# One shared transpose for two heads' 64-key tails, values of the tails against zero-padded V, and a planner that prices each change of product kind

## The chip, the cores and the metric

The kernel runs on one core of a Trainium2 chip. The metric is the device time of one execution in microseconds (us). The engines are PE (TensorE, matrix products and transposes), PEld (its weight loads), DVE (VectorE), ACT (ScalarE), POOL (GpSimd) and SP (SyncE, whose queue issues all DMAs here).

## The reference

Block-causal attention over 4 batches, 8 heads, 576 positions and 64 dimensions per head, with blocks of 64 keys, and two feed-forward layers behind it:

```python
scores = scale * np.matmul(q, k.transpose(0, 1, 3, 2))
block_i = pos[:, None] // block          # block = 64
block_j = pos[None, :] // block
scores = np.where(block_i >= block_j, scores, -1000000000.0)
scores = scores - np.max(scores, axis=-1, keepdims=True)
attn = np.exp(scores)
attn = attn / (np.sum(attn, axis=-1, keepdims=True) + 1e-09)
attn_out = np.matmul(attn, v)
...
x = np.ascontiguousarray(attn_out.transpose(0, 2, 1, 3)).reshape(B * S, H * D)   # 2304 x 512
x = _moe_ref(x=x, **moe_kwargs)      # h = x @ w_in; g piecewise quadratic in h; g @ w_out, d_ff = 2048
return _moe2_ref(x=x, **moe2_kwargs) # h = x @ w_in; g = max(0.01 h, h); g @ w_out
```

## The kernel before

**Attention in units.** Two heads make a pair (16 pairs). A pair's 576 queries are split into part "a" (the first 320) and part "b" (the last 256), so there are 32 units, 16 of each part. Inside a unit the queries stand in chunks, `CH = (first query, queries, keys)`: chunks 0, 1, 2 of part a see 64, 192 and 320 keys, chunks 3 and 4 of part b see 448 and 576. Every number of keys is an odd multiple of 64, so each chunk and head ends in a tail of 64 keys that doesn't fill 128 rows. In the first chunk the tail is all there is.

**A unit's steps.** `unit_scores` loads q and k (and the values V), multiplies q by the scale on POOL, and forms scores on PE (line L651). The contraction is over 64 dimensions, so head 0 uses rows 0 to 63 of the array and head 1 rows 64 to 127 side by side. `softmax` masks (L564), takes maxima (L566) on DVE and exponentials on ACT (L573). The probabilities lie with queries on partitions, so `unit_values` transposes them in pieces of 128 keys on PE (L743), copies the result from PSUM to SBUF on ACT (L748) or DVE (L750), and multiplies it with V on PE (L770). There the output has 64 columns for each head, so the two heads use the two halves of the array's columns side by side. For the first four units the division by the row sum is made late, by a broadcast product with the identity (L762). A chunk whose keys don't fill a multiple of 128 has its last 64 columns zeroed by POOL (L667) and its tail transposed as a full piece, for each head apart. `PCOL` says where each chunk's probabilities begin, `TILES` which pieces share one PSUM slot and one copy, `SUMS` which piece meets which columns of the result:

```python
TILES = {"a": [[(0, 0), (1, 0), (2, 0)], [(1, 1), (2, 1), (2, 2)]],
         "b": [[(3, 0), (4, 0), (3, 1), (4, 1)], [(3, 2), (4, 2), (3, 3), (4, 3)], [(4, 4)]]}
SUMS = {"a": [(0, 0, 0, 320), (1, 0, 64, 256), (1, 256, 192, 128)], ...
```

So an a unit has 12 transposes, two copies (640 and 768 columns) and 6 value products, a b unit 18 transposes, three copies (1024, 1024 and 256 columns) and 10 value products. A score or value product in float32 has two rows in the trace, a transpose one.

**Three kinds of product on PE.** Whole-array products (the feed-forward layers' and the transposes), scores (row halves) and values (column halves). The code calls the last two `tiled`.

**The rest.** While attention runs, `h1_block` and `h1_wide` (L877, L887, L855) fill PE with the first layer's products on tokens whose attention is done, w_float (L508 to L523) and `conv_unit` (L925 to L943) unpack and prepare weights on ACT, DVE and POOL. Then come the other products with seven sub-products to a block: L1191 and L1252 (first layer's output), L1068 (second layer's first product), L1252 again (second layer's output).

**What sets the order.** Nothing runs in the order in which it is written. Every step is an `Op` with an engine, a cost in ns and its dependencies. `Plan.schedule` simulates the engines 400 times with random disturbances (`SEED`), keeps the order whose simulated end is earliest, and emits it; each engine then runs its own list in order. PE pays `ENTRY = 105` in this model when it goes from whole-array to tiled products. Where `SLACKS` isn't 0, a product of the kind that PE is in may be taken ahead of one of the other kind. In the first 20 us, expected gaps of PE are filled with products of zeros (L545), after ten such products at the start.

Of the kernel before, what the change touches and what calls it, by code (L numbers as in the profile page):

```python
# [25 lines left out]
SA = 320  # L26
# [41 lines left out]
ENTRY = 105  # L68
SLACKS = (0, 800)
SEED, TRIES = 6, 400  # L70
# [85 lines left out]
class Op:  # L156
    __slots__ = ("eng", "cost", "prio", "fn", "deps", "succ", "need", "ready", "seq", "end", "start", "port", "tiled", "lag")


class Plan:  # L160
# [9 lines left out]
    def op(self, eng, cost, prio, fn, r=(), w=(), port=False, tiled=False, lag=0):  # L170
        o = Op()
        o.port, o.tiled, o.lag = port, tiled, lag
# [33 lines left out]
    def forward(self, prio, slack):  # L206
# [8 lines left out]
        tiled = False  # L215
# [6 lines left out]
        while events:  # L222
# [5 lines left out]
            for e in engines:  # L228
                if free[e] <= t and waiting[e]:
# [3 lines left out]
                    if e == "PE":  # L233
                        if slack and o.tiled != tiled and waiting[e]:
                            other = min((x for x in waiting[e] if ops[x[1]].tiled == tiled), default=None)
# [61 lines left out]
    def late(self, done, extra):  # L297
# [5 lines left out]
        port, tiled = 0, False  # L303
        for o in done:
# [12 lines left out]
            if e == "PE":  # L317
                if o.tiled and not tiled:
                    t += ENTRY
                tiled = o.tiled  # L320
# [52 lines left out]
def fused_kernel(ctx, tc, qk, v, w1, w2, out):  # L373
# [36 lines left out]
    def pe(cost, prio, fn, r, w, tiled=False):  # L410
        plan.op("PE", cost, prio, fn, r, w, tiled=tiled)
# [142 lines left out]
    def softmax(prio, tag, s, parts, late=None):  # L554
# [5 lines left out]
        for c, heads, view, _, _ in ((p[0], p[2], p[3], p[4], p[5]) for p in parts):  # L560
            keys = CH[c][2]
            m = len(heads)
            if c > 0:
                dve(64 * m, prio, lambda view=view, keys=keys: nc.vector.memset(  # L564
                    view()[0:64, :, keys - 64:keys], NEG), [], [s], fixed=60)
# [36 lines left out]
    PCOL = {0: 0, 1: 128, 2: 384, 3: 0, 4: 512}  # L602
    units = {}
    padded = {}
    ROOMS = {0: {"p": [(P1, 0)], "v": (P2, 1536), "qk": (P2, 2560)},
             1: {"p": [(P2, 0)], "v": (P2, 2176), "qk": (P2, 3392)},
             2: {"p": [(C[8], 0), (C[9], 0)], "v": (C[8], 1152), "qk": (C[10], 0)},
             3: {"p": [(C[11], 0)], "v": (C[12], 0), "qk": (C[12], 384)},
             4: {"p": [(C[13], 0), (C[14], 0)], "v": (C[13], 1152), "qk": (C[15], 0)}}

    def unit_scores(pair, part, prio, ring, room_):
# [5 lines left out]
        nv, nqk, npr = (640, 832, 1152) if part == "b" else (384, 640, 768)  # L617
        vt = vs.reg(vo, nv, shape=lambda ap: ap.rearrange("p (j d) -> p j d", d=128))
        if len(own["p"]) == 1:
            ps_, po = own["p"][0]  # L620
            pr = [ps_.reg(po, 2 * npr)] * 2
            part_of = lambda hd, a, e: (pr[hd], (2000 * hd + a, 2000 * hd + e))
            prob = lambda hd, a, e: pr[hd].get()[:, npr * hd + a:npr * hd + e]
        else:
            pr = [ps_.reg(po, npr) for ps_, po in own["p"]]
            part_of = lambda hd, a, e: (pr[hd], (a, e))
            prob = lambda hd, a, e: pr[hd].get()[:, a:e]
# [4 lines left out]
        q0, k0, nq, nk, nj = (SA, 0, SA, SA, 3) if part == "a" else (0, SB, SB, S, 5)  # L632
        x = qk_room[0].reg(*qk_room[1:])
        if part == "a":
            dma(128 * 2 * SA * 4, prio - 8, lambda: nc.sync.dma_start(
                x.get()[:, 0:2 * SA].rearrange("p (c s) -> p c s", c=2), qk[pair][:, :, SB:]), [], [x])
        else:
            dma(128 * 832 * 4, prio - 8, lambda: nc.sync.dma_start(
                x.get(), qk[pair].rearrange("p c s -> p (c s)")[:, 0:832]), [], [x])
# [783 lines left out]
```

## Time and profile before

| | us |
|---|---|
| median of 3 runs | 928.32 (928.02 to 935.54) |
| the profiled execution | 928.28 |
| its span, first to last instruction | 926.5 |
| PE busy in it | 915.6 |
| DVE, ACT, POOL busy | 727.7, 519.6, 293.9 |

The time of an execution has 1.78 us around the span. Engines work side by side, so their busy times don't add up; an engine's busy share says how much of the span it had something to do, and where it is near 100% its own work sets the time. The granted clock of TensorE is 1.000 over the whole span.

### The profile page before, as it was taken

What the parts mean: (1) busy time and instruction counts of PE and PEld (TensorE: products, weight loads), DVE (VectorE), ACT (ScalarE), POOL (GpSimd) and SP (SyncE); (2) the same over time, 40 slices, a digit from 0 to 9 for tenths busy, and PEclk for the clock granted to TensorE, in tenths of its full rate; (3) what the DMA queues carried; (4) which work ended last, traced back from release to release, by engine and by line L of the source; (5) the groups of instructions that cost most, each with busy time, mean ns of one, the idle gap of its engine ahead of it and who ended that gap; (6) DMA issues with size and microseconds to landing.
All of it is one profiled execution on the core that took longest, in us unless ns stands there. A gap on an engine that the chain in (4) does not pass through costs nothing.

```text
span 926.5 us, 18684 instructions
## 1 busy us (share of the span) xinstructions
PE 915.6 (99%) x6818; PEld 827.7 (89%) x6818; DVE 727.7 (79%) x1247; ACT 519.6 (56%) x1014; POOL 293.9 (32%) x490
## 2 busy tenths in 40 slices
PE   9999999999999999999999999999999999999998
PEld 6687887876777878899999999999999999999998
DVE  6998677777777646559989798677879899888977
ACT  7788677787777666653434343344535664434333
POOL 5577787787665400000000040146445000000000
PEclk9999999999999999999999999999999999999999
DMA  8678788788799789656525499987887983544433
GB/s 310 212 224 249 236 281 285 261 275 272 273 315 323 276 263 325 191 172 209 154 84 161 140 348 337 346 290 269 266 279 242 328 269 91 176 132 139 148 91 115
DMA packets 164892, 216.72 MB, mean 234 GB/s; under 512 B 9920, under 2 KB 138432, under 8 KB 164800
## 3 DMA queue, kind: packets, MB, share of 16 engines
q1 hardware_dynamic: 164800, 215.52, 71.8%
q8 instruction: 54, 0.88, 0.4%
q14 instruction: 38, 0.31, 0.1%
HBM read 134.74 MB, written 80.74 MB: 233 GB/s over the span
## 4 chain that ended last, share of the span: by engine, by line
PE 92%; DVE 2%; DMA 2%; ACT 1%; issue 1%; POOL 1%; SPq 0%; POOLq 0%; DVEq 0%; ACTq 0%
PE bank L1252 31%; PE bank L1068 15%; PE bank L855 14%; PE bank L887 7%; PE bank L1191 6%; PE slot L651 5%; PE slot L770 5%; PE slot L743 5%; DMA rg<-gd 1%; DVE ra L976 1%; DMA wcd<-rg 1%; DMA rb<-x1d 1%; ACT rp L573 1%; PE bank L545 1%; PE slot L762 0%
## 5 line engine op out<-in xcount | busy, mean ns | idle before, releaser
L1068 PE MATMUL bank<-rp,w 128*128 128x288 f32 x1344 | 179.7, 294 | 1.2 <-ACT ra L978 0.9
L1068 PEld LDWEIGHTS bank<-rp,w 128*128 128x128 f32 x1344 | 178.1, 188 | 1.8 <-ACT ra L978 1.2
L976 DVE TENSOR_TENSOR ra<-ra,bank 128x288 f32<-128x288 f32 (+2 forms) x280 | 125.8, 488 | 43.7 <-ACT ra L978 21.8
L1252 PE MATMUL bank<-w,rp 128*128 128x256 f32 x1014 | 145.9, 277 | 0.0
L1252 PEld LDWEIGHTS bank<-w,rp 128*128 128x128 f32 x1014 | 129.8, 188 | 0.0
L855 PE MATMUL bank<-ra,w 128*128 128x512 f32 x384 | 100.0, 398 | 0.3 <-DVE rg L838 0.3
L1237 ACT ACTIVATE rp<-ra 128x1024 fp32r<-128x1024 f32 (+1 forms) x48 | 47.5, 991 | 72.5 <-DVE ra L1211 62.7
L855 PEld LDWEIGHTS bank<-ra,w 128*128 128x128 f32 x384 | 70.1, 188 | 17.1 <-issue 2.3
L838 DVE SCALAR_TENSOR_TENSOR rg<-bank,rg 128x512 f32<-128x512 f32 x72 | 49.3, 684 | 38.0 <-ACT rg L837 35.1
L1072 ACT ACTIVATE ra<-ra 128x1152 f32<-128x1152 f32 x32 | 37.3, 1167 | 71.4 <-DVE ra L976 71.4
L1252 PE MATMUL bank<-rp,w 128*128 128x256 f32 x508 | 76.6, 279 | 0.0
L936 POOL TENSOR_TENSOR w<-w 128x128 f32<-128x128 f32 x128 | 66.9, 543 | 26.7 <-DVE w L932 24.7
L1003 POOL TENSOR_TENSOR xs<-xs,rp 128x576 f32<-128x576 f32 x1 | 1.5, 1547 | 212.0 <-DMA xs<-x2d 212.0
L836 ACT ACTIVATE rg<-bank 128x512 f32<-128x512 f32 x72 | 43.1, 598 | 43.2 <-PE bank L855 36.6
L1252 PEld LDWEIGHTS bank<-rp,w 128*128 128x128 f32 x508 | 67.2, 188 | 0.0
L1240 DVE TENSOR_TENSOR rb<-ra,rp 128x1024 fp32r<-128x1024 f32 (+1 forms) x48 | 54.3, 1133 | 3.9 <-ACT rp L1237 0.7
L1252 PE MATMUL bank<-w,rb 128*128 128x256 f32 x294 | 57.0, 277 | 0.0
L887 PE MATMUL bank<-ra,w 128*128 128x256 f32 x352 | 53.6, 289 | 0.0
L855 PE MATMUL bank<-rb,w 128*128 128x512 f32 x192 | 53.1, 398 | 0.0
L887 PEld LDWEIGHTS bank<-ra,w 128*128 128x128 f32 x352 | 45.1, 188 | 3.5 <-issue 2.6
L1252 PE MATMUL bank<-rg,w 128*128 128x256 f32 x280 | 47.7, 279 | 0.0
L1236 ACT ACTIVATE rp<-rp 128x768 fp32r<-128x768 f32 (+1 forms) x33 | 26.4, 803 | 36.2 <-DMA rp<-gd 21.5
(169 smaller groups left out, 1977.6 us busy)
## 6 DMA issues: line engine op xcount, KB each, us to landing
rp<-gd SPq DMA_DIRECT2D x41, 512.0 KB, 4.2
wcd<-w SPq DMA_DIRECT2D x43, 448.0 KB, 4.6
gd<-ra SPq DMA_DIRECT2D x32, 576.0 KB, 4.8
gd<-rg SPq DMA_DIRECT2D x64, 256.0 KB, 3.6
w<-wcd SPq DMA_DIRECT2D x32, 512.0 KB, 5.7
w<-wcd SPq DMA_DIRECT2D x32, 384.0 KB, 5.7
w<-w SPq DMA_DIRECT2D x44, 256.0 KB, 4.6
w<-w SPq DMA_DIRECT2D x16, 512.0 KB, 5.1
```

Of the source, the lines that this page charges most:

```text
L651: nc.tensor.matmul(out, lhsT=x.get()[r, q:q + 128], rhs=x.get()[r, k0 + ka:k0 + kb], start=start, stop=True, skip_group_check=True)
L743: nc.tensor.transpose(s.get()[:, hd, o:o + 128], prob(hd, a, a + 128), ident.get())
L838: dve(512, pv, lambda: nc.vector.scalar_tensor_tensor(gt.get(), ps.get(), 1.0, gt.get(), op0=ALU.max, op1=ALU.min), [ps, gt], [gt])
L855: nc.tensor.matmul(ps.get(), lhsT=win(fc, c, kc), rhs=xview(xt, x, kc), start=(k == 0 and kc == 0), stop=(k == 2 and kc == NKC - 1), skip_ ...
L887: nc.tensor.matmul(ps.get()[:, 256 - j * 256:512 - j * 256], lhsT=win(fc, c, kc), rhs=xview(xt, x, kc), start=(k == 0 and kc == 0 and j == 0),
L936: plan.op("POOL", 430, prio, lambda o=o, a=a, b=b, op=op: nc.gpsimd.tensor_tensor(sl(o), sl(a), sl(b), op=op), [(fx, (a, a + 1)), (fx, (b, ...
L976: dve(cols, prio, lambda: nc.vector.tensor_tensor(out(o), out(a), P[b][1](), op=op), [P[b][0], (slots, (a, a + 1))], [(slots, (o, o + 1))])
L1068: nc.tensor.matmul(ps.get()[:, 0:HALF], lhsT=wc(1, p, cw, li, 128 * kc, 128 * kc + 128), rhs=r.get()[:, cx, kc], start=(k == 0 and kc == 0 ...
L1191: nc.tensor.matmul(ps[t].get()[:, 0:n], lhsT=wc(z, p, cw, li, 128 * t, 128 * t + 128), rhs=x.get()[:, n * zi:n * zi + n], start=(p == 0 an ...
L1237: act(4 * n, pv, lambda tt=tt, ht=ht: nc.scalar.activation(s_(ht, 0, 4), s_(tt, 0, 4), AF.Copy), [tt], [ht], sb=True)
L1240: dve(4 * n, pv, lambda tt=tt, ht=ht, lt=lt: nc.vector.tensor_tensor(s_(lt, 0, 4), s_(tt, 0, 4), bc(s_(ht, 0, 4)), op=ALU.subtract), [tt, ...
L1252: nc.tensor.matmul(ps.get()[:, 256 * t:256 * t + w], lhsT=b if wide else g, rhs=g if wide else b, start=(p == 0 and k == 0 and t == 0), st ...
```

## The change

Head 1's keys are stored in reversed order of blocks, from the host on. Its tail then is the first 64 keys instead of the last, and stands behind head 0's tail in the probabilities, which now lie head beside head for each chunk (`PBASE`). One transpose of 128 columns takes both tails: rows 0 to 63 of the result are head 0's, 64 to 127 head 1's. The tails' value products (`ENDS`) run over all 128 rows, against V that is zero in the other head's rows, so that each head takes only its own. The zeroing of pad columns goes away. The a unit has 9 transposes (6 of `MAINS`, 3 of `TAILS`), copies of 768 and 320 columns and 10 value products; the b unit 16 transposes, two copies of 1024 columns and 12 value products, with the same total of columns as before in both. V comes in two layouts, with 5 blocks of 64 KB for an a unit instead of 3, and 6 for a b unit instead of 5; q and k come in one contiguous piece for each unit.

The planner knows three kinds of product (`mode` 0 whole array, 1 scores, 2 values), pays for each change into a kind, has new costs for the three steps, may take products of the present kind up to 3000 ns ahead of others, and starts from another seed.

```diff
-ENTRY = 105
-SLACKS = (0, 800)
-SEED, TRIES = 6, 400
+SWITCH = (98, 190, 142)
+SLACKS = (0, 1000, 3000)
+SEED, TRIES = 7, 400
...
-                        if o.tiled and not tiled:
-                            o.end += ENTRY
-                        tiled = o.tiled
+                        if o.mode != mode:
+                            o.end += SWITCH[o.mode]
+                        mode = o.mode
...
-    PCOL = {0: 0, 1: 128, 2: 384, 3: 0, 4: 512}
+    PBASE = {0: 0, 1: 128, 2: 512, 3: 0, 4: 896}
...
-        nv, nqk, npr = (640, 832, 1152) if part == "b" else (384, 640, 768)
+        nv, nqk = (768, 832) if part == "b" else (640, 640)
...
+            k = k0 + hd * (nk - CH[c][2])
+            nc.tensor.matmul(out, lhsT=x.get()[r, q:q + 128], rhs=x.get()[r, k + ka:k + kb], start=start, stop=True,
...
-        for c in ((0, 1, 2) if part == "a" else (3, 4)):
-            keys = CH[c][2]
-            a, b_ = PCOL[c] + keys, PCOL[c] + (keys + 127) // 128 * 128
-            for hd in range(2):
-                if a == b_ or padded.get(room_) == part:
-                    continue
-                pool(0, prio - 1, lambda a=a, b_=b_, hd=hd: nc.gpsimd.memset(prob(hd, a, b_), 0.0), [], [part_of(hd, a, b_)], fixed=86)
...
+    MAINS = {"a": [[(1, 0, 0), (2, 0, 128), (2, 1, 256)], []],
+             "b": [[(3, 0, 0), (4, 0, 128), (3, 1, 256), (4, 1, 384)], [(3, 2, 0), (4, 2, 128), (4, 3, 256)]]}
+    TAILS = {"a": [[], [(0, 0, 0), (1, 0, 64), (2, 0, 192)]], "b": [[], [(3, 0, 384), (4, 1, 384)]]}
+    SUMS = {"a": [(0, 0, 0, 64, 256), (1, 0, 256, 192, 128)],
+            "b": [(0, 0, 0, 0, 256), (1, 0, 256, 0, 256), (2, 1, 0, 0, 256), (3, 1, 256, 128, 128)]}
+    ENDS = {"a": [(2, 0, 0, 0, 64), (3, 0, 64, 64, 128), (4, 0, 192, 192, 128)],
+            "b": [(4, 0, 384, 0, 128), (5, 1, 384, 128, 128)]}
...
-                for hd in range(2):
-                    o = 0
-                    for c, j in blocks:
-
-                        a = PCOL[c] + 128 * j
-                        nc.tensor.transpose(s.get()[:, hd, o:o + 128], prob(hd, a, a + 128), ident.get())
-                        o += CH[c][1]
-            pe(2 * m * 0.85 + 15, prio, f, [*dict.fromkeys(pr), ident], [s])
+                for c, b, o in tails:
+                    a = CH[c][2] - 64
+                    nc.tensor.transpose(s.get()[:, b, o:o + 128], prob(c, a, a + 128), ident.get())
+                for c, j, o in mains:
+                    keys = CH[c][2]
+                    for hd in range(2):
+                        a = keys + 64 + 128 * (keys // 128 - 1 - j) if hd else 128 * j
+                        nc.tensor.transpose(s.get()[:, hd, o:o + 128], prob(c, a, a + 128), ident.get())
+            pe((n + 127) // 128 * 109 + 10, prio, f, [*dict.fromkeys(pr.values()), ident], [s])
...
+            for z, h, o, q0, m in ENDS[part]:
+                for hd in range(2):
+                    r = slice(64 * hd, 64 * hd + 64)
+                    nc.tensor.matmul(s.get()[r, 0, q0:q0 + m], lhsT=vt.get()[:, z, r], rhs=pts[1].get()[:, h, o:o + m], start=False,
+                                     stop=True, skip_group_check=True)
+        pe(sum(max(x[4], 100) for x in SUMS[part] + ENDS[part]) * 1.68 + 10, prio, f, [vt] + pts, [s], 2)
...
-    EVAC = {"a": ("act", "dve"), "b": ("act", "dve", "act")}
+    EVAC = {"a": ("act", "dve"), "b": ("act", "dve")}
...
+    for z in range(2):
+        ends[:, :, z, :, z] = vv[:, :, 0, :, z]
```

Line numbers move by one or two. In the changed kernel tails are transposed in L737, whole pieces in L742; value products are L767 (`SUMS`) and L772 (`ENDS`), scores L652, products of zeros L544.

**An a unit on PE, beside the first layer's products.** In the rows, slot is a PSUM slot of attention, bank one of the first layer, rp and w are SBUF rooms. Before, the unit's second group of transposes and its values:

```order
L743 MATMUL slot_128<-ident,rp_1_95 128x128 x6
L887 MATMUL bank_90<-ra_1_934,w_1_891 128x256 x4
L887 MATMUL bank_90<-rb_1_881,w_1_891 128x256 x2
L887 MATMUL bank_90<-rb_1_1158,w_1_891 128x256 x2
L887 MATMUL bank_90<-ra_1_934,w_1_891 128x256 x8
L651 MATMUL slot_128<-w_1_201 128x320 x2
L770 MATMUL slot_129<-rp_1_78,rp_1_95 64x320 x2
L770 MATMUL slot_129<-rp_1_78,rp_1_95 64x256 x2
L770 MATMUL slot_129<-rp_1_78,rp_1_95 64x128 x2
```

Now, at the same stage:

```order
L737 MATMUL slot_112<-ident,rp_1_91 128x128 x3
L888 MATMUL bank_89<-ra_1_944,w_1_680 128x256 x8
L888 MATMUL bank_89<-rb_1_857,w_1_680 128x256 x2
L888 MATMUL bank_89<-rb_1_1137,w_1_680 128x256 x2
L767 MATMUL slot_127<-rp_1_165,rp_1_91 64x256 x2
L767 MATMUL slot_127<-rp_1_165,rp_1_91 64x128 x2
L772 MATMUL slot_127<-rp_1_165,rp_1_91 64x64 x2
L772 MATMUL slot_127<-rp_1_165,rp_1_91 64x128 x4
L652 MATMUL slot_112<-w_1_208 128x320 x2
```

The second group has three transposes instead of six, and the values end in a product of 64 and two of 128 columns.

**A b unit on PE at the same stage.** Before, from its first transposes to its values:

```order
L743 MATMUL slot_129<-ident,rp_1_78 128x128 x8
L887 MATMUL bank_90<-rb_1_881,w_1_638 128x256 x2
L887 MATMUL bank_90<-rb_1_1158,w_1_638 128x256 x2
L743 MATMUL slot_145<-ident,rp_1_78 128x128 x8
L887 MATMUL bank_90<-ra_1_934,w_1_638 128x256 x4
L743 MATMUL slot_128<-ident,rp_1_78 128x128 x2
L887 MATMUL bank_90<-ra_1_934,w_1_638 128x256 x4
L887 MATMUL bank_90<-rb_1_881,w_1_638 128x256 x2
L887 MATMUL bank_90<-rb_1_1158,w_1_638 128x256 x2
L651 MATMUL slot_145<-w_1_155 128x448 x2
L770 MATMUL slot_129<-rp_1_78,rp_1_95 64x256 x8
L770 MATMUL slot_129<-rp_1_78,rp_1_95 64x128 x2
```

Now:

```order
L742 MATMUL slot_111<-ident,rp_1_165 128x128 x8
L888 MATMUL bank_89<-ra_1_944,w_1_488 128x256 x4
L737 MATMUL slot_112<-ident,rp_1_165 128x128 x2
L742 MATMUL slot_112<-ident,rp_1_165 128x128 x6
L888 MATMUL bank_89<-ra_1_944,w_1_488 128x256 x4
L888 MATMUL bank_89<-rb_1_857,w_1_488 128x256 x2
L888 MATMUL bank_89<-rb_1_1137,w_1_488 128x256 x2
L888 MATMUL bank_89<-ra_1_944,w_1_488 128x256 x4
L652 MATMUL slot_111<-w_1_120 128x448 x2
L767 MATMUL slot_127<-rp_1_165,rp_1_91 64x256 x6
L767 MATMUL slot_127<-rp_1_165,rp_1_91 64x128 x2
L772 MATMUL slot_127<-rp_1_165,rp_1_91 64x128 x4
```

The third group of two transposes and its slot are gone, and two of the four tails' transposes with them.

**The opening on PE,** where wz marks the products of zeros and late the late division. Before:

```order
L545 MATMUL bank_90<-wz 128x128 x5
L651 MATMUL slot_128<-rp_1_95 128x320 x2
L743 MATMUL slot_129<-ident,rp_1_95 128x128 x6
L545 MATMUL bank_90<-wz 128x128 x2
L743 MATMUL slot_145<-ident,rp_1_95 128x128 x6
L545 MATMUL bank_90<-wz 128x128 x2
L762 MATMUL slot_128<-ident,latea_198 64x64 x2
L762 MATMUL slot_128<-ident,latea_198 64x128 x4
```

Now:

```order
L544 MATMUL bank_88<-wz 128x128 x6
L652 MATMUL slot_111<-rp_1_91 128x320 x2
L742 MATMUL slot_112<-ident,rp_1_91 128x128 x6
L544 MATMUL bank_88<-wz 128x128 x2
L737 MATMUL slot_127<-ident,rp_1_91 128x128 x3
L544 MATMUL bank_88<-wz 128x128 x2
L652 MATMUL slot_112<-w_1_139 128x64 x2
L652 MATMUL slot_112<-w_1_139 128x192 x2
L652 MATMUL slot_127<-w_1_139 128x320 x2
L759 MATMUL slot_111<-ident,latea_182 64x64 x2
L759 MATMUL slot_111<-ident,latea_182 64x128 x4
L544 MATMUL bank_88<-wz 128x128 x3
```

The third unit's scores stand ahead of the first late division, and there are 23 products of zeros in all where there were 21.

**Counts over the whole order of PE.** Transposes 480 before, 400 now; value products 256 and 352; all other products as many as before. Runs of scores, each entered from another kind: 56 and 46. Runs of values or late divisions: 36 and 36. Returns to whole-array products: 55 and 56.

## Rows read from the trace of the kernel before

**Rows 1.** The page, busy time and share of the span of each engine.

```profile
PE 915.6 (99%) x6818; PEld 827.7 (89%) x6818; DVE 727.7 (79%) x1247; ACT 519.6 (56%) x1014; POOL 293.9 (32%) x490
```

**Rows 2.** Stretches, busy us of PE, PEld, DVE, ACT, POOL, granted clock, DMA share, GB/s.

```profile
0.00:6.50 6.50, 5.45 (x30) 5.22 (x32) 0.17 (x1) 1.49 (x2) 2.92 (x23) 1.00 0.64 185
6.50:46.00 39.50, 36.72 (x298) 26.51 (x296) 36.62 (x76) 33.31 (x111) 22.05 (x37) 1.00 0.82 274
46.00:330.00 284.00, 282.38 (x2021) 218.05 (x2020) 211.78 (x398) 214.32 (x562) 197.99 (x334) 1.00 0.83 270
330.00:747.00 417.00, 415.20 (x2938) 402.42 (x2937) 325.47 (x531) 195.98 (x253) 70.94 (x96) 1.00 0.76 246
747.00:926.50 179.50, 175.89 (x1539) 175.51 (x1538) 153.69 (x244) 74.53 (x89) 0.00 (x0) 1.00 0.46 142
```

**Rows 3.** What PE waited for after 46 us: us in total, times, longest.

```profile
PE slot L743 <- ACT rp L573: 1.1, 1, 1.1
PE bank L1068 <- ACT ra L978: 0.9, 1, 0.9
PE slot L651 <- POOL w L641: 0.6, 1, 0.6
PE slot L651 <- ACT rp L748: 0.6, 1, 0.6
```

**Rows 4.** The chain that ended last, its end: start us, us, what.

```profile
922.93 0.42 DVE ra L976
```

**Rows 5.** Groups of PE by line: transposes (of two groups alike but for the room).

```profile
L743 PE MATMUL slot<-ident,rp 128*128 128x128 f32 x252 | 33.8, 276 | 1.4 <-ACT w L573 0.9 <-ACT rp L573 0.2 <-issue 0.2
```

**Rows 6.** The chain in 196 to 216 us, a stretch where PE never waits.

```profile
199.49 0.75 PE slot L651 x8
...
202.46 0.92 PE bank L855 x4
203.38 0.74 PE slot L651 x4
204.12 1.34 PE slot L770 x12
...
207.50 1.96 PE slot L743 x18
...
210.39 0.95 PE slot L651 x4
211.34 2.10 PE slot L770 x20
213.44 1.12 PE bank L855 x4
```

**Rows 7.** The chain in 12 to 30 us, the opening.

```profile
12.60 0.45 PE bank L545 x4
...
16.52 0.64 PE bank L545 x4
...
25.09 0.85 PE slot L762 x12
```

**Rows 8.** DVE's and ACT's copies from PSUM in 46 to 330 us, by form.

```profile
L750 DVE COPY rp<-slot 128x1024 f32<-128x1024 f32 x15 | 18.4, 1224 | 9.5 <-PE slot L743 9.2
L750 DVE COPY rp<-slot 128x768 f32<-128x768 f32 x12 | 11.4, 948 | 3.8 <-PE slot L743 3.6
...
L748 ACT COPY rp<-slot 128x256 f32<-128x256 f32 x15 | 5.6, 376 | 0.7 <-PE slot L743 0.7
```

**Rows 9.** DMA issues, V's loads: KB each, median us to landing.

```profile
rp<-v SPq DMA_DIRECT2D x8, 320.0 KB, 4.3
...
rp<-v SPq DMA_DIRECT2D x9, 192.0 KB, 4.3
```

**Rows 10.** Two stretches with the fullest DMA, columns as in group 2.

```profile
150.00:167.00 17.00, 16.43 (x135) 13.29 (x136) 11.81 (x23) 12.53 (x37) 13.60 (x24) 1.00 0.90 293
713.00:747.00 34.00, 32.81 (x247) 32.35 (x246) 30.86 (x59) 21.09 (x27) 2.63 (x5) 1.00 0.94 313
```

More of the change, by code (lines that the diff above doesn't have):

```diff
@@ L156 @@
 class Op:
-    __slots__ = ("eng", "cost", "prio", "fn", "deps", "succ", "need", "ready", "seq", "end", "start", "port", "tiled", "lag")
+    __slots__ = ("eng", "cost", "prio", "fn", "deps", "succ", "need", "ready", "seq", "end", "start", "port", "mode", "lag")
 class Plan:
@@ L233, in forward @@
                     if e == "PE":
-                        if slack and o.tiled != tiled and waiting[e]:
-                            other = min((x for x in waiting[e] if ops[x[1]].tiled == tiled), default=None)
+                        if slack and o.mode != mode and waiting[e]:
+                            other = min((x for x in waiting[e] if ops[x[1]].mode == mode), default=None)
                             if other is not None and other[0] <= first[0] + slack:
@@ L317, in late @@
             if e == "PE":
-                if o.tiled and not tiled:
-                    t += ENTRY
-                tiled = o.tiled
+                if o.mode != mode:
+                    t += SWITCH[o.mode]
+                mode = o.mode
             if o.port:
@@ L372, in fused_kernel @@
 @with_exitstack
-def fused_kernel(ctx, tc, qk, v, w1, w2, out):
+def fused_kernel(ctx, tc, qka, qkb, va, vb, w1, w2, out):
     nc = tc.nc
@@ L408, in turn, with pe @@
         return places[i % len(places)]
[L410 to L411 removed]
+    def pe(cost, prio, fn, r, w, mode=0):
+        plan.op("PE", cost, prio, fn, r, w, mode=mode)
     def act(cols, prio, fn, r, w, sb=False, extra=0):
@@ L559, in softmax @@
         i = 0
-        for c, heads, view, _, _ in ((p[0], p[2], p[3], p[4], p[5]) for p in parts):
+        for c, o, heads, view, _, _ in parts:
             keys = CH[c][2]
@@ L563, in softmax, with masked @@
             if c > 0:
-                dve(64 * m, prio, lambda view=view, keys=keys: nc.vector.memset(
-                    view()[0:64, :, keys - 64:keys], NEG), [], [s], fixed=60)
+                def masked(o=o, keys=keys, heads=heads):
+                    if len(heads) == 1:
+                        a = o if heads[0] else o + keys - 64
+                        return flat2(s)[0:64, a:a + 64]
+                    a, d = o + keys - 64, 576 - keys
+                    return flat2(s)[0:64, a:a + 2 * d].rearrange("p (h t) -> p h t", h=2)[:, :, 0:64]
+                dve(64 * m, prio, lambda masked=masked: nc.vector.memset(masked(), NEG), [], [s], fixed=60)
             dve(keys * m, prio, lambda view=view, i=i, m=m: nc.vector.tensor_reduce(
@@ L643, in unit_scores @@
         ready = [x]
-        dma(128 * nj * 512, prio + 20, lambda: nc.sync.dma_start(vt.get()[:, 0:nj], v[pair][:, 0:nj]), [], [vt])
+        dma(128 * nj * 512, prio + 20, lambda: nc.sync.dma_start(vt.get(), (va if part == "a" else vb)[pair]), [], [vt])
         def score(out, c, hd, ka, kb, start):
@@ L685, in f @@
                         score(s.get()[:, hd, o:o + CH[c][2]], c, hd, 0, CH[c][2], i == 0)
-            pe(score_cost(sum(CH[c][2] for c, _ in grp)), prio, f, ready, [s], True)
+            pe(score_cost(sum(max(CH[c][2], 128) for c, _ in grp)), prio, f, ready, [s], 1)
             softmax(prio, f"{n}_{grp[0][0]}", s, [
@@ L728, in unit_values @@
         pts = []
-        for i, blocks in enumerate(TILES[part]):
+        for i, (mains, tails) in enumerate(zip(MAINS[part], TAILS[part])):
             s = slot(ring[0])
             ring.append(ring.pop(0))
-            m = sum(CH[c][1] for c, _ in blocks)
-            pT = P1.reg(4352 if i == 2 else turn("pt", (2304, 3328)), 256 if i == 2 else 1024,
-                        shape=lambda ap: ap.rearrange("p (h t) -> p h t", h=2))
+            pT = P1.reg(turn("pt", (2304, 3328)), 1024, shape=lambda ap: ap.rearrange("p (h t) -> p h t", h=2))
@@ L757, in f @@
             def f():
-                for i, c in enumerate((0, 1, 2) if part == "a" else (3, 4)):
+                for i, c in enumerate(EVERY[part]):
                     r = CH[c][1]
```

101 lines of the change are left out of this document (51 added, 50 removed).

## The prediction

> **What bounds the kernel now.** I read the page's busy times first, then the same by stretches, then what PE waited for, then the chain. PE is busy for 99% of the span, DVE for 79%, ACT for 56% [rows 1]. The stretches say where this holds: from 46 to 747 us PE is busy for 697.6 of 701 us at a granted clock of 1.00 [rows 2], and its two longest waits there are 1.1 and 0.9 us [rows 3]. Until 46 us things stand differently: from 6.5 to 46 us DVE is busy for 36.62 of 39.5 us, and the 36.72 us of PE contain products of zeros, which do nothing [rows 2]. The end is fixed: the last product is done about 922.5 us after the start, then a sum on DVE begins at 922.93 [rows 4] and the stores follow, so that of the 3.6 us without PE after 747 us most is this tail [rows 2]. So a microsecond of PE work taken out between 46 and 330 us, where attention stands between other products, is a microsecond of the end, as long as the products that follow find their data. One taken out of the opening may turn into waiting.
>
> **The change part by part.**
>
> *Transposes.* 18 in a row after whole-array products take 1.96 us in the chain [rows 6], 0.109 us each (their durations of 276 ns overlap [rows 5]). The order has 400 instead of 480: 80 x 0.109 = 8.7 us less on PE, 3 per a unit and 2 per b unit.
>
> *Value products.* The two sizes of units give the price of a column (of both heads side by side) and of the change of kind: 2.10 us for 1152 columns and 1.34 us for 704 [rows 6] are 0.76/448 = 1.70 ns a column, and leave 0.14 us for the entry. The total of columns stays. What is new is the product of 64 columns in each a unit, and more short ones. A product of 128 columns was in both sums and they fit one price, so I price it by its columns. For 64 columns there are two rows, and they disagree. Scores with 64 + 192 columns take 0.75 us, with 448 columns 0.95 us, with 320 columns 0.74 us [rows 6]. Less 1.70 ns a column the latter two leave 0.19 and 0.20 us for the entry; the first leaves 0.75 - 0.435 = 0.31 us, so its product of 64 columns costs 0.12 us more than its columns. The late division has products of 64, 128 and 128 columns in the array's column halves and takes 0.85 us [rows 7]: 0.544 us of columns and an entry of 0.14 leave 0.17 us, and in that lies a change of kind inside the group (its first product contracts over 64 rows, the others over 128), for which the other changes cost 0.14 to 0.20. So nothing is left there for a short product. The bounds are 0 and 0.12 us per a unit, 0 to 1.9 us in all. I take 0, because the late division has the values' column halves and the scores don't.
>
> The Trainium skill ("TensorE: Matmul & The Clock Gate", section "LDWEIGHTS (loading the stationary operand)") says that a weight load takes as many cycles of 1.2 GHz as it has columns. By an estimate from that page two heads' loads of 64 columns, one behind the other, would take 107 ns for each half of a float32 product, and a product of 64 columns would cost twice its columns, 1.7 us in all and a result of 920.3 us with the other terms of the sum below. Its two loads of 128 columns would then take 213 ns in the scores, or 0.43 us for the product of 64, where the row has 0.23 us; so the trace agrees with the rule at most for loads that lie side by side.
>
> *Changes of kind.* Counted in the two orders, entries into scores fall from 56 to 46, at 0.195 us: 1.95 us less. Entries into values stay at 36. Returns go from 55 to 56, at 1.12 - 0.92 = 0.20 us [rows 6]: 0.2 us more. Together 1.75 us less.
>
> *Copies from PSUM.* An a unit's copy on DVE shrinks from 768 to 320 columns: from 948 ns, with 1.08 ns a column between the two forms, to an estimated 465 ns, 0.48 us less [rows 8]. That is 7.7 us of DVE over 16 units. On ACT it grows by 128 columns, and in a b unit a copy of 376 ns goes [rows 8]. After 46 us both lie beside PE (DVE busy 75%, ACT 75% of 46 to 330 us [rows 2]) and are worth nothing by themselves. What is late next is the copy ahead of a b unit's values: the last one had 256 columns on ACT, 376 ns, and now has 1024 on DVE, 1224 ns [rows 8]. In the order shown scores of 448 columns and eight products of the first layer or more stand between, and the first three value products read only the other copy, so I cost it at nothing; where no cover stands, it is 0.85 us for a unit.
>
> *Zeroing, q and k.* 36 small POOL instructions go, and the loads of q and k become one piece of the same size. POOL is busy for 70% of 46 to 330 us [rows 2] and PE waited for it once, 0.6 us [rows 3], so nothing.
>
> *V's loads.* An a unit loads 320 KB instead of 192, a b unit 384 instead of 320 [rows 9]: 16 x 192 KB = 3.1 MB more, issued from SP's queue with all the rest, where loads and stores of the first layer stand behind them. At 293 GB/s [rows 10] that is 10.7 us of transfers if nothing else ran; hidden while DMA has room (share 0.83 in 46 to 330 us [rows 2]). I cost it at nothing and make the other end a rival.
>
> *The opening.* Four a units and one or two b units are transposed before 46 us, 1.5 to 1.7 us of the 8.7. There PE waits for others, and the expected gaps are filled: 21 products of zeros before, 23 now, 0.45 to 0.64 us for two [rows 7]. For a loss speaks that the order has two more of them. Against it speaks that DVE, busy for 93% of that stretch, loses 4 x 0.48 = 1.9 us of copies. Ends: 0 and 1.6 us lost. I take half, 0.8 us.
>
> *Sum.* -8.7 - 1.75 + 0 + 0.8 = -9.65 us against the profiled execution's 928.28 us, which is the median of the runs within 0.04: **918.6 us**. PE's other idle time, 3.4 us from 46 to 747 us [rows 2], I let stand. The whole order is new, so each of them may go and others come.
>
> **The rivals.**
>
> *Short value products are dear.* If each costs what the scores' one does, and the opening keeps nothing, the sum is -8.7 - 1.75 + 1.9 + 1.6 = -6.95: 921.3 us. For it: the only row of a product of 64 columns by itself in a longer group is the scores'. Against it: the late division. The Trainium skill's rule on weight loads, cited above, speaks for this case.
>
> *New waits.* The order was made by a model from other costs, and a b unit's values wait for a copy that is 0.85 us longer. If that copy is bare in five of 16 units, 4.2 us come back: 922.8 us. Against it: PE waited for a copy once, 0.6 us [rows 3].
>
> *More than the sum.* The opening is DVE's, shortens by the whole 1.9 us of its copies, and the longest wait of PE, 1.1 us [rows 3], goes too: -8.7 - 1.75 - 0.3 - 1.1 = -11.85, 916.4 us.
>
> *V's bytes make DMA the bound: slower than before.* In 46 to 330 us 270 GB/s x 284 us = 76.7 MB move [rows 2]; with some 2.5 MB more (the units loaded after 46 us) it is 79.2 MB in 276 us, 287 GB/s. If the queue gives no more than the 270 of now, the stretch lasts 293 us instead of 276, and the time is 918.6 + 17 = 935.6 us; below 277 GB/s it is slower than before. For it: with DMA at 0.90 and 293 GB/s PE lost 0.57 us in 17. Against it: that is more than 287, and 313 GB/s were moved in 713 to 747 us [rows 10].
>
> That the change doesn't do what it says is no case: the order has the 80 transposes less.
>
> **How the numbers follow.** Forecast 0.58, short products dear 0.11, new waits 0.15, more than the sum 0.11, DMA 0.05. A measurement of this kernel tells a change of about 1%, 9.3 us, from none: below 919.0 us is faster, above 937.6 slower. The forecast lies 0.4 us inside faster; of its 0.58, spread over some 1.5 us to each side, I count 0.36 as faster and 0.22 as same. More than the sum is faster; dear products and new waits are the same. Of the DMA case 0.03 is slower, the rest same. Together faster 0.47, same 0.50, slower 0.03. The likeliest single case gives 918.6 all the same. The range goes from 916.0, which takes in the case of more, to 923.0, which takes in that of new waits; beyond lie the worse half of new waits and DMA.
>
> **What would show it.** Right: L737 and L742 have 400 rows with about 0.109 us from one to the next; an a unit's values take 1.34 us in the chain, a b unit's 2.10; PE stays at 99% in 46 to 321 us, and the end of attention (the last L772) and everything behind it come some 10 us earlier; DVE's copies are 465 ns. Wrong: values of 1.46 us in an a unit (short products); waits of L767 or L772 for L748 (copies); PE idle behind loads, or a DMA share of 0.90 with waits (bytes); a start of the first layer's products in the opening that is no earlier, or new idle time at 390 or 745 us, where the new order is free to place it.

## The result, and the profile after

| | before | changed |
|---|---|---|
| median, us | 928.26 (4 executions) | 918.70 (4 executions, 918.52 to 923.09) |
| ratio, 95% interval | | 0.9898 (0.9867 to 0.9929) |
| median of a second set, us | 928.95 (23 executions) | 919.04 (6 executions, 917.89 to 920.30) |
| its ratio | | 0.9884 (0.9860 to 0.9908) |

The change takes 9.6 us off, where 9.65 were forecast. The first profiled execution of the changed kernel is the one of 923.09 us; a second one took 917.89 us, and the rows are from the second where nothing else is said. Why the first took 5 us more is told in the last section: for most of its last stage the same products ran at another rate.

The page of the changed kernel, busy time and share of the span (915.9 us), answers to [rows 1]:

```profile
PE 904.9 (99%) x6934; PEld 826.4 (90%) x6934; DVE 722.6 (79%) x1247; ACT 515.5 (56%) x998; POOL 291.4 (32%) x454
```

PE is busy for 10.7 us less, and its share is as before. The same stretches as in [rows 2], with the same columns:

```profile
0.00:6.50 6.50, 5.45 (x40) 5.12 (x40) 0.82 (x5) 1.49 (x2) 1.62 (x8) 1.00 0.62 184
6.50:46.00 39.50, 35.94 (x312) 25.86 (x309) 34.77 (x77) 34.76 (x111) 24.97 (x30) 1.00 0.84 298
46.00:330.00 284.00, 282.72 (x2163) 226.03 (x2162) 210.85 (x397) 214.16 (x553) 195.55 (x316) 1.00 0.86 284
330.00:747.00 417.00, 415.82 (x2983) 404.88 (x2982) 331.36 (x544) 196.61 (x252) 69.27 (x101) 1.00 0.76 250
```

The opening leaves PE idle for 3.56 us of 39.5 instead of 2.78 (3.09 in the first profiled execution). From 46 to 330 us PE is idle for 1.28 us instead of 1.62, though DMA's share rose from 0.83 to 0.86. The chain in the same 20 us as [rows 6], which now hold an a and a b unit:

```profile
196.28 1.29 PE slot L652 x12
197.57 0.80 PE slot L767 x8
198.37 0.55 PE slot L772 x12
198.92 1.13 PE bank L856 x4
200.05 0.87 PE slot L742 x8
200.93 0.93 PE bank L856 x4
201.86 0.22 PE slot L737 x2
202.08 0.66 PE slot L742 x6
...
203.66 0.95 PE slot L652 x4
204.61 1.67 PE slot L767 x16
206.28 0.44 PE slot L772 x8
...
214.11 0.33 PE slot L737 x3
```

The b unit's 16 transposes take 0.87 + 0.22 + 0.66 = 1.75 us, 0.109 each as before. The a unit's values take 0.80 + 0.55 = 1.35 us (1.34 before), the b unit's 1.67 + 0.44 = 2.11 (2.10). So the new value products cost what their columns cost, the ones of 64 columns included. The first row shows one of the entries that went: both groups of an a unit's scores stand in one run with one entry, 1.29 us, where before they were two of 0.75 and 0.74 us [rows 6]. That prices the entry once more, at 0.20 us.

The copies on DVE and on ACT in 46 to 330 us, as in [rows 8]:

```profile
L748 DVE COPY rp<-slot 128x1024 f32<-128x1024 f32 x16 | 19.5, 1220 | 8.4 <-PE slot L742 8.4
L748 DVE COPY rp<-slot 128x320 f32<-128x320 f32 x12 | 5.8, 485 | 4.1 <-PE slot L737 2.5 <-ACT rp L577 1.5
...
L746 ACT COPY rp<-slot 128x1024 f32<-128x1024 f32 x15 | 15.2, 1015 | 4.5 <-PE slot L742 4.5
...
L746 ACT COPY rp<-slot 128x768 f32<-128x768 f32 x12 | 9.6, 803 | 3.6 <-PE slot L742 3.6
```

The a unit's copy on DVE took 485 ns, where 465 were estimated. A b unit's values wait for the longer copy once:

```profile
PE slot L767 <- DVE rp L748: 0.3, 1, 0.3
```

For the comparisons below one point is of use: the start of the last of the first layer's 512-column products. All of attention lies before it (its last value product starts at 329.1 us before and at 315.9 us now), and the last stage, where executions of one kernel differ, lies behind it. The view of one source line gives it as the last start; of the kernel before:

```profile
L855 PE MATMUL bank<-rb,w x192: 387/392/505, 206.4 to 396.2; 128*128 128x512 f32 x192
```

and of the changed kernel:

```profile
L856 PE MATMUL bank<-rb,w x192: 387/392/505, 200.7 to 386.7; 128*128 128x512 f32 x192
```

396.2 us became 386.7 (387.1 in the first profiled execution): 9.5 us by there, the gain of the medians. The last sum on DVE begins at 912.09 us instead of 922.93 [rows 4], which is 1.3 us more; the waits of L1068 before, 0.9 and 0.3 us [rows 3], are not there in this execution, and the first one has one of 0.9 us again.

### The profile page after: what moved, and what is told of

Its sections match the earlier page's. It is cut to its first block, busy times and chain, and to the rows that moved or that the text cites. A ratio compares the mean times of both kernels' runs of the same rounds, so it can differ in the third digit from the quotient of the medians.

```text
span 921.0 us, 18843 instructions
## 1 busy us (share of the span) xinstructions
PE 908.6 (99%) x6934; PEld 829.8 (90%) x6934; DVE 721.4 (78%) x1247; ACT 515.5 (56%) x998; POOL 292.9 (32%) x454
## 4 chain that ended last, share of the span: by engine, by line
PE 86%; DMA 5%; DVE 4%; ACT 2%; issue 2%; POOL 1%; SPq 0%; DVEq 0%; ACTq 0%
PE bank L1253 30%; PE bank L1069 16%; PE bank L856 13%; PE bank L1192 6%; PE bank L888 6%; PE slot L652 5%; PE slot L767 3%; PE slot L742 3%; DMA gd<-ra 2%; PE slot L772 1%; ACT rp L577 1%; PE slot L737 1%; DVE ra L977 1%; DMA w<-w 1%; DMA rp<-gd 1%
## 5 line engine op out<-in xcount | busy, mean ns | idle before, releaser
L977 DVE TENSOR_TENSOR ra<-ra,bank 128x288 f32<-128x288 f32 (+2 forms) x280 | 125.9, 490 | 47.9 <-ACT ra L979 18.5
L1253 PE MATMUL bank<-w,rp 128*128 128x256 f32 x1014 | 148.4, 280 | 0.1
L1253 PEld LDWEIGHTS bank<-w,rp 128*128 128x128 f32 x1014 | 132.1, 189 | 0.4 <-DVE rp L1239 0.3
L1253 PE MATMUL bank<-rp,w 128*128 128x256 f32 x508 | 75.3, 279 | 0.0
L937 POOL TENSOR_TENSOR w<-w 128x128 f32<-128x128 f32 x128 | 63.7, 516 | 30.6 <-DVE w L933 14.2
L1253 PEld LDWEIGHTS bank<-rp,w 128*128 128x128 f32 x508 | 66.5, 188 | 0.0
L1253 PE MATMUL bank<-w,rb 128*128 128x256 f32 x294 | 56.4, 279 | 0.0
L1253 PE MATMUL bank<-rg,w 128*128 128x256 f32 x280 | 46.2, 279 | 0.8 <-ACT rg L1238 0.8
```

Source lines behind the costliest of these rows:

```text
L937: plan.op("POOL", 430, prio, lambda o=o, a=a, b=b, op=op: nc.gpsimd.tensor_tensor(sl(o), sl(a), sl(b), op=op), [(fx, (a, a + 1)), (fx, (b, ...
L977: dve(cols, prio, lambda: nc.vector.tensor_tensor(out(o), out(a), P[b][1](), op=op), [P[b][0], (slots, (a, a + 1))], [(slots, (o, o + 1))])
L1253: nc.tensor.matmul(ps.get()[:, 256 * t:256 * t + w], lhsT=b if wide else g, rhs=g if wide else b, start=(p == 0 and k == 0 and t == 0), st ...
```

## The experiments

The theory: PE's work up to that point sets the time, and the change takes from it 80 transposes at 0.109 us and ten entries into scores at 0.195 us. The rivals: the new planner, its order or its seed is what brings the gain; DVE's relief is; new costs (short products, V's bytes) take part of it back.

| kernel | median, us | start of the last 512-column product of the first layer (below: their end), us | entries into scores, returns |
|---|---|---|---|
| before | 928.26 | 396.2 | 56, 55 |
| changed | 918.70 | 386.7 (387.1) | 46, 56 |
| tails twice | 927.32 | 395.2 | 46, 56 |
| ends split | 919.19 | 387.8 | 46, 56 |
| planner alone | 933.17 | 398.6 | 55, 63 |
| products alone | 927.97 | 391.7 | 57, 67 |
| before, seed 7 | 937.74 | 401.3 | 56, 64 |
| changed, seed 6 | 923.44 | 388.3 | 49, 55 |
| no price for a change of kind | 932.25 | 391.7 | 58, 80 |
| measured prices | 923.92 | 390.2 | 47, 57 |
| copies swapped | 922.44 | 388.7 | 46, 56 |
| V twice to one place | 1002.33 | 471.5 | 46, 56 |
| V once more to a spare place | 925.38 | 395.2 | 46, 56 |

The kernel before took 928.6 to 928.95 us (medians of 18 to 25 executions) beside these.

### Transposes, in an unchanged order

```diff
-                for c, b, o in tails:
+                for c, b, o in tails + tails:
```

> The changed kernel in its own order, with each of the 80 transposes of tails made twice, to the same place. Nothing else is touched, the planner's costs included. If a transpose costs 0.109 us on the path, the time is 918.7 + 8.7 = 927.4 us, or down to 926.6 us where those of the opening fall into waits. If transposes lie beside other work or the gain came from the order, it stays within 2 us of 918.7.

927.32 us, 8.6 more than the changed kernel, and the first layer's products end 8.1 us later than in its first profiled execution. The chain of this kernel at the a unit's and the b unit's tails:

```profile
199.90 0.65 PE slot L737 x6
...
207.06 0.44 PE slot L737 x4
```

Six in place of three take 0.65 us, four in place of two 0.44. With the same order and the same copies, 80 transposes cost 8.1 to 8.6 us. Followed from product to product, this execution is 1.1 us behind the changed kernel's at 46 us, with 14 of them done twice, and 7.7 us at 330 us, with all 80: 6.6 us for the 66 behind the opening, 0.10 us each, so these lie on the path with nearly their whole price, and those of the opening with a part of it. The rest, 0.4 to 0.8 us, is lost between 330 us and the point. The executions go from 925.50 to 933.38 us, and the profiled one is the slowest, with 172 products in 20 us throughout the last stage, so the point is the better measure here.

### Short value products, in an unchanged order

```diff
-            for z, h, o, q0, m in ENDS[part]:
+            for z, h, o, q0, m in [(z, h, o + i, q0 + i, 64) for z, h, o, q0, m in ENDS[part] for i in range(0, m, 64)]:
```

> The changed kernel in its own order, with each tail's value product of 128 columns split into two of 64, so 64 splits in all and 144 products of 64 columns for each pair of heads instead of 16. If a value product costs its columns, 1.70 ns each, the time stays at 918.7 us (within 1 us). If a product of 64 columns costs 0.12 us more than its columns, as in the scores, it is 918.7 + 128 x 0.12 = 934.1 us.

919.19 us: 0.5 us for 64 splits (0.7 to 1.1 at the point). In its chain the a unit's ends, now ten products instead of six, and the b unit's:

```profile
199.30 0.58 PE slot L772 x20
...
207.24 0.46 PE slot L772 x16
```

0.55 became 0.58 us, 0.44 became 0.46. A product of 64 columns costs 0.01 us more than its columns, not 0.12. The rival falls. Weight loads of 64 columns set no floor here, so the rule of the Trainium skill that the prediction weighed ("TensorE: Matmul & The Clock Gate", section "LDWEIGHTS (loading the stationary operand)") holds in this place at most for two heads' loads side by side.

### The planner's part and the products' part, each alone

Planner alone: the kernel before with `SWITCH`, the three modes, the new costs, seed and slacks.

> The kernel before with the planner's part of the change alone: prices for each change of kind, new costs of scores, transposes and values, the new seed and slacks. The products are those of before. The order that comes out has 55 entries into scores (56 before), 63 returns to whole-array products (55) and 36 entries into values (36). If the sum of the prediction holds (the gain is the 80 transposes and fewer changes of kind), this gives no gain: -0.2 + 1.6 us for the entries, 929.7 us, with some 2 us to each side for new waits. If the gain came from the planner and the new order, it is 920 us or less.

Products alone: the changed kernel with `ENTRY`, the old costs, seed and slacks.

> The changed kernel with the planner of before: the old price for an entry, old constants in the costs, old seed and slacks. The shared transposes and zero-padded V stay. Its order has 57 entries into scores, 67 returns and 35 into values. By the sum: -8.7 us of transposes, +0.2 + 2.4 - 0.1 us for the entries, +0.8 in the opening, so 928.3 - 5.4 = 922.9 us. If the planner brought the gain, 927 us or more; if the entries cost nothing and the order doesn't matter, 919 to 920 us.

The planner alone gives no gain: 933.17 us. The first layer's products end 2.4 us later than before, where the counts said 1.4; the last stage of its profiled execution, one of 937.79 us, has the other rate throughout. The products alone end there 4.5 us earlier, where the counts said 5.4; but the whole comes out at 927.97 us, no gain to speak of and 5 us over what was expected. So an order with 11 more entries and 11 more returns gives half of the gain back by that point. Where the other 4 us went, the windows of its last stage say (columns as in [rows 2]):

```profile
780.00:800.00 20.00, 20.00 (x173) 20.00 (x171) 17.20 (x27) 7.67 (x9) 0.00 (x0) 1.00 0.49 155
840.00:860.00 20.00, 20.00 (x172) 20.00 (x172) 15.59 (x21) 7.52 (x8) 0.00 (x0) 1.00 0.43 119
870.00:890.00 20.00, 20.00 (x179) 20.00 (x178) 16.98 (x23) 8.48 (x9) 0.00 (x0) 1.00 0.48 147
```

172 products in 20 us, then 179, with PE busy throughout: the other rate, for some 105 us.

The two runs also allow what neither does alone, a comparison of the products with the planner held. Under the new planner, with its seed, they bring the point from 398.6 to 386.7 us: 11.9 us, where the counts say 8.7 for the transposes, 1.75 for nine entries and 1.4 for seven returns, 11.9 in all, less some 0.7 us for three more products of zeros. Under the old one they bring 4.5 us. So in these orders the change needs both of its parts, and how much the products bring depends on the order as well.

### The price of a change of kind, and the luck of an order

```diff
-SWITCH = (98, 190, 142)
+SWITCH = (0, 0, 0)
```

> The changed kernel with the three prices for changes of kind set to 0, all else kept. Its order has 58 entries into scores (46), 80 returns (56) and 36 into values (36). At 0.195 us an entry and 0.20 us a return that is 2.3 + 4.8 = 7.1 us more: 925.8 us, and the first layer's products end at 394 us instead of 387.1. If changes of kind are hidden or cheap, within 2 us of 918.7.

By the end of the first layer's products 4.6 to 5.0 us are lost, not 7.1. The direction is right and the size a third less, but that doesn't show a lower price: up to that point PE is idle for 4.8 us here and for 6.9 (6.7 in the first execution) in the changed kernel, so some 2 us of the 7.1 can be hidden by waits that this order doesn't have. The median is 932.25 us; behind the point the profiled execution, 933.26 us, has waits in the second layer and the other rate in most of its last stage:

```profile
PE bank L1069 <- ACT ra L979: 2.6, 3, 1.6
PE bank L1069 <- DVE ra L977: 0.7, 1, 0.7
...
840.00:860.00 20.00, 20.00 (x172) 20.00 (x171) 15.41 (x22) 8.24 (x9) 0.00 (x0) 1.00 0.40 111
```

```diff
-SEED, TRIES = 7, 400
+SEED, TRIES = 6, 400
```

> The changed kernel with the seed of before, all else kept, so another order by the same rules. It has 49 entries into scores (46 in the changed kernel), 55 returns (56), 35 entries into values (36) and 26 products of zeros (23). If the gain is products and entries, +0.6 - 0.2 - 0.1 us and up to 0.7 us for the zeros: 918.7 to 920 us, and the first layer's products end within 1.5 us of 387.1. If it was a lucky order, 923 us or more.

The kernel before with seed 7 instead of 6, and nothing else:

> The kernel before with the seed of the change (7) and nothing else. Its order has 56 entries into scores (56 before), 64 returns (55) and 36 into values (36): 9 x 0.20 = 1.8 us more, 930.1 us, and the first layer's products end at 398 us instead of 396.2. If the seed is what was lucky, 924 us or less.

The changed kernel with `SWITCH = (200, 200, 150)` and `TRIES = 800`:

> The changed kernel whose planner pays the prices read in the trace (200 ns for a return to whole-array products instead of 98, 200 for scores, 150 for values) and tries 800 orders instead of 400, same seed. Its order has 47 entries into scores (46), 57 returns (56) and 35 into values (36), so the same within 0.3 us: 918.7 us, the first layer's products end within 1 us of 387.1. If the price of a return was what still cost time, 916 us or less.

All three are later than their counts say: the first layer's products end at 388.3 us (387.0 to 387.7 by the counts), 401.3 (398) and 390.2 (some 387), and the medians are 923.44, 937.74 and 923.92 us. Paying the measured price of a return doesn't help: its order has as many returns, and more waits in the opening, where PE is busy for 38.89 us up to 46 us, against 41.39 in the changed kernel. So orders by the same or nearly the same rules differ by 1 to 5 us at that point, and both given kernels have the best of the orders seen for their products. The old products took 928 to 938 us in three orders, the new ones under the new planner 919 to 932 in four.

### DVE's relief

The two copies of an a unit swapped in what is emitted (the planner's order stays):

> The changed kernel with the two copies of an a unit swapped between the engines: 768 columns on DVE as before the change, 320 on ACT; the order of PE is the same. It gives back the 0.48 us that DVE had saved in each a unit, 7.7 us in all. If copies lie beside PE after 46 us, only the four units of the opening count: 918.7 to 920.6 us. If DVE's relief was part of the gain all along, 922 us or more.

The first layer's products end 1.6 to 2.0 us later. PE's idle time up to 46 us is 4.25 us instead of 4.61 (4.14 in the first execution), so the opening isn't where it went. From 46 to 330 us it is 2.26 instead of 1.28 us, which is half of it:

```profile
46.00:330.00 284.00, 281.74 (x2156) 224.42 (x2155) 213.38 (x397) 208.04 (x552) 197.24 (x317) 1.00 0.86 282
```

Idle time misses a part of each pause: a transpose's row is 0.27 us long, and the next one starts 0.109 us behind it, so 0.16 us of a pause between them leave no gap. Followed from product to product, which stand in the same order, this execution is 0.3 us behind the second one of the changed kernel at 46 us and 2.0 us at 330 us. So the relief was worth up to 2 us, as a little less waiting among the units and not in the opening, and the expectation got the sum at this point right for the wrong place. The swap is not quite the arrangement of before: there DVE made the second of the two copies, here the first. The median, 922.44 us, is 3.7 us up and would fall under the other alternative; its profiled execution has 172 products in 20 us in the last stage.

### V's bytes

```diff
...
+            for _ in range(2):
+                nc.sync.dma_start(vt.get(), (va if part == "a" else vb)[pair])
...
```

> The changed kernel with every load of V issued twice in a row to the same place: 11.3 MB more on SP's queue (16 x 320 KB + 16 x 384 KB), nearly four times what the change adds, in the same order of all engines. If V's bytes lie in what DMA has left, as the prediction costed them, the time stays within 1 us of 918.7. If DMA is at its limit in attention, up to 11.3 MB / 293 GB/s = 38 us come on top; at a quarter of that, 928 us, the change's own 3.1 MB would have cost some 2.6 us.

1002.33 us, 83.6 more, far beyond the bytes. The queue of SP says why; us in total, times, longest:

```profile
SPq L646 <- DMA rp<-va: 47.2, 9, 8.3
SPq L646 <- DMA rp<-vb: 43.0, 8, 6.8
SPq L646 <- DMA w<-vb: 35.4, 8, 6.0
SPq L646 <- DMA w<-va: 33.2, 7, 5.6
```

The second load writes where the first does, so it waits at the head of the queue until the first has landed, 5 us each time for all 32, and everything behind it waits as well. Up to 471.5 us PE is idle for 61.4 us, and the granted clock there is 0.94 on the mean, between its two levels of 1.2 and 2.4 GHz, where the changed kernel has 1.00; so a part of the 83.6 us is TensorE's clock. The run measured a wait at the head of the queue and not bytes. The same bytes without the wait:

```diff
...
+            nc.sync.dma_start(spare, (va if part == "a" else vb)[pair].rearrange("p j d -> p (j d)"))
...
```

> The changed kernel with V's 11.3 MB read once more from HBM into spare places of HBM that nothing reads: right behind each load of V in SP's queue, without a wait between the two. Unlike two loads to the same place, this adds bytes and issues alone. If V's bytes lie in what DMA has left, the time stays within 2 us of 918.7 and the first layer's products end at 387 to 389 us. If bytes cost their time at some 293 GB/s, 38 us come on top; if two loads to one place were dear because of their wait and not of their bytes, this one is far below their 1002 us.

925.38 us, 6.7 more than the changed kernel, and all of it is lost by the end of the first layer's products, which is 8.1 to 8.5 us later (395.2 us). Its windows of the opening and of attention, columns as in [rows 2]:

```profile
6.50:46.00 39.50, 36.70 (x320) 26.41 (x319) 35.10 (x78) 34.21 (x109) 25.18 (x29) 1.00 0.96 354
46.00:330.00 284.00, 277.49 (x2127) 220.91 (x2126) 204.78 (x393) 208.24 (x545) 196.39 (x317) 0.99 0.90 307
```

At a share of 0.90 and 307 GB/s PE is idle for 6.5 us instead of 1.3. Its longest wait, 2.0 us for a copy on ACT, goes back to a load of weights that `conv_unit` unpacks; ACT stands at this load with attention's exponentials and copies behind it:

```profile
162.58 8.66 DMA w<-w
...
171.32 0.04 ACT w L932
...
171.89 1.11 ACT w L577 x4
173.00 0.91 ACT rp L751
...
173.96 1.02 PE slot L657 x4
```

The load took 8.66 us to land. Loads w<-w of 256 KB take 5.8 us at the median here and 4.5 in the changed kernel, those of 512 KB 7.0 and 5.6. So the DMA rival is a real mechanism, and not far off: 11.5 MB (11.3 in the expectation), read and written again with 32 more issues, cost some 8 us, and the change's own 3.1 MB, at a share of 0.86, none that the windows show. In proportion, by an estimate, they would be worth 2.3 us.

### The changed kernel once more

> The changed kernel as it is, once more, for a second profiled execution. The first one took 923.1 us where the others took 918.5 to 918.8, with the last stage's products of 256 columns 117.8 ns apart for 115 us and 113.3 ns for the rest. If that is a matter of the execution and not of the kernel, the executions fall near 918.6 or near 923 again, attention and the first layer's products end at the same times (387.1 us), and only the stretch behind 740 us differs.

Six executions of 917.89 to 920.30 us. At the point above the two profiled executions agree within 0.4 us. Behind it they don't: the first one has a wait of 0.9 us for DVE between 600 and 747 us, and then the other rate.

## Why the prediction was right, point by point

*The sum.* 918.6 us was forecast, 918.70 and 919.04 are the two medians, and the mechanism is the one that was forecast: less work on PE up to the end of the first layer's products. That they agree within 0.1 us is luck in part. The opening and the waits missed their terms by some tenths of a us each way, other orders by the same or nearly the same rules were 1 to 5 us later at the point, and the prediction knew nothing of the two rates of the last stage; the execution that had the lower one for 115 us took 923.09 us, just beyond the range's end of 923.0.

*Transposes, -8.7 us.* Right: 0.109 us each in the changed kernel, and 8.1 to 8.6 us for 80 in an unchanged order, of which 7.7 us come with the transposes themselves.

*Short products, 0 of 0 to 1.9 us.* Right, shown by the split ends: 0.01 us each. The row of the late division was the nearer one; the scores' 0.12 us isn't the values'.

*Changes of kind, -1.75 us.* Right in sign. The price of an entry is borne out by an a unit's two groups of scores in one run (0.20 us less than in two). The order with 36 more changes lost a third less than their price, with some 2 us less waiting, so it bounds the price and doesn't measure it: no new order changes the kinds alone.

*The opening, +0.8 us of 0 to 1.6.* Two more products of zeros (0.45 us at the least) and 0.78 us more idle time (0.31 in the first execution): some 0.8 to 1.2 us lost, within the bounds and at or a little over the half that I took. The argument that DVE's shorter copies would speak against a loss there was not borne out: PE waits for exponentials on ACT in the opening (L737 and L759, some 1.7 us in all), and swapping the copies cost next to nothing there.

*Copies and zeroing, 0.* The longer copy ahead of a b unit's values is waited for once, 0.3 us. The prediction let three value products of a b unit stand before that wait; by `SUMS` only two read the other copy alone, the third reads the copy on DVE. What DVE saved was worth up to 2 us in attention by the swap, which the prediction costed at nothing. Against the kernel before, PE's idle time from 46 to 330 us fell by 0.34 us, which balances what the opening lost more.

*V's bytes, 0 with a rival of 17 us.* Right: no more idle time in attention. The rival's threshold was set too late: I had it at 277 to 293 GB/s of what the queue can give, but 307 GB/s were moved with PE waiting, so what counts is when a transfer lands that an engine stands at (8.66 us for one load there), not the mean rate.

*Other waits unchanged.* This was the weakest step, and held: PE's idle time from 46 to 747 us is 2.46 us (3.42 before), but 4.21 us in the first profiled execution. Three other orders show that it needn't have held: 0.6 to 3.5 us more by the end of the first layer's products than their counts say. New waits deserved more than the 0.15 that they got, all the more because of the two rates below.

*The signs.* Of those named, the 400 rows of L737 and L742, the prices of values and the share of 99% came as said. The end of attention came 13.2 us earlier and not some 10, since the new order puts more of the first layer's products behind it; what follows came some 10 us earlier.

## What to carry to other kernels

Where one engine is busy for 99% of a stretch, a change can be priced by counting its instructions in the emitted order and reading each one's step from a run of equal ones; to test such a price, repeat the instruction in an unchanged order, because every new order costs or gives some microseconds of its own. Where a search sets the order, compare several seeds of both versions, or a point inside the program before which all of the change lies, and not two totals alone. A queue whose head waits for a transfer costs far more than the bytes: 5 us for each load here.

## What the runs showed of the hardware that I had not expected

The same products run at one of two rates, with PE busy throughout and a granted clock of 1.00, its level of 2.4 GHz. The last stage (L1253, 256 columns and one weight load each) in two stretches of the first profiled execution of the changed kernel, 923.09 us:

```profile
800.00:820.00 20.00, 20.00 (x172) 20.00 (x171) 14.76 (x22) 8.09 (x9) 0.00 (x0) 1.00 0.29 83
870.00:890.00 20.00, 20.00 (x179) 20.00 (x178) 17.29 (x26) 8.22 (x10) 0.00 (x0) 1.00 0.42 122
```

and of the second, 917.89 us:

```profile
800.00:820.00 20.00, 20.00 (x179) 20.00 (x178) 16.15 (x23) 7.19 (x8) 0.00 (x0) 1.00 0.36 106
870.00:890.00 20.00, 20.00 (x179) 20.00 (x178) 14.78 (x23) 7.91 (x10) 0.00 (x0) 1.00 0.35 102
```

172 or 179 products in 20 us, 4% apart; the starts of neighbours are 117.8 or 113.3 ns apart, without a value between. DMA's share doesn't set it: in the first execution the lower rate stands at shares of 0.29 (800 to 820 us) and of 0.59 (820 to 840 us), the higher one at 0.42. DVE doesn't slow down with PE: its sums of 512 columns (L977) take 0.68 us at either rate. The profiled execution of the kernel before has the higher rate in nearly all of the last stage, as the second one of the changed kernel has, so the gain read from these two doesn't come from the rate:

```profile
800.00:820.00 20.00, 20.00 (x179) 20.00 (x178) 16.62 (x25) 8.41 (x10) 0.00 (x0) 1.00 0.44 128
```

Nor does a rate belong to an execution: the same line with the same columns makes the first layer's output from 442 to 562 us, and there the second execution, its last stage at the higher rate, has the lower one:

```profile
480.00:500.00 20.00, 20.00 (x172) 20.00 (x171) 18.44 (x27) 9.26 (x10) 0.00 (x0) 1.00 0.53 155
```

Over 1500 products of the last stage the difference comes to 6.8 us, and over the first execution's 115 us at the lower rate to 4.4 us of the 5.2 between the two here. Nearly all times of the kernel before fall into two groups, 927.5 to 929.8 and 933 to 935.5 us, about as far apart; as no execution of the upper group was profiled, that the rate makes the groups is likely and not shown. The change from one to the other stands at places where the flow of products breaks for a moment (a product held up by 80 ns at 867.7 us turned the first execution to the higher rate), but other such breaks change nothing, and I found no rule. No run tried to force it, so what decides between the two rates stays open.
